# Alibi attention and feed-forward on one core: q and k of the last nine blocks turned by transposing DMA

## The chip, the core and the metric

The kernel runs on one core of one Trainium2 chip. The core has five engines with instruction queues of their own: TensorE (PE in the profile; its weight loads are shown as PEld), VectorE (DVE), ScalarE (ACT), GpSimd (POOL) and SyncE (SP). SP does no arithmetic here; it issues DMAs and runs its queue strictly in order, as every engine does. POOL issues the loads that change the type from fp32 to fp16 on the way, and computes two tiny operations a block. Sixteen DMA engines move the data for all queues.

The metric is the time of one execution on the device, in microseconds (us). The kernel before took 323.11 us, the median of three runs (322.46 to 323.45).

## The reference

For 8 batches, 8 heads, 576 positions and a head width of 64 the reference computes sliding-window attention with linear position biases, joins the heads to rows of 512, and puts each row through a normalisation and a two-layer network with a residual:

```python
scores = scale * np.matmul(q, k.transpose(0, 1, 3, 2))
bias = slopes[:, None, None] * (-np.abs(rel).astype(np.float32))[None, :, :]
mask = (rel >= 0) & (rel < window)               # window = 128
scores = np.where(mask, scores + bias[None], -1000000000.0)
attn = softmax(scores)                           # over the keys
x = matmul(attn, v) -> (batch, 576, 512)
xn = (x - mean) / np.sqrt(var + 1e-06) * g_ln
out = x + np.maximum(xn @ w_ch1, 0.0) @ w_ch2    # 512 -> 2048 -> 512
```

## The kernel before

**Blocks.** Two batches form a pair, p = 0 to 3. A pair has nine blocks of 128 rows: blocks 0 to 7 are positions 0 to 511, alternately of the one and the other batch, and block 8 (T) holds the last 64 positions of both. In the order of work the 36 blocks are numbered n = 9p + blk. The last nine, n = 27 to 35, are those of pair 3.

**Attention of a block.** POOL loads raw q and k of two blocks at a time (load_qk, L207 to L218) and v of one (load_v, L220). A partition of the raw tile takes two neighbouring positions, so that a piece read is 512 bytes. For the scores q and k must lie with the head's 64 elements on the partitions. That is what `turn(p, i)` does (L283): TensorE transposes 64 by 64 pieces into PSUM (L277; 64 of them for two blocks, 32 for a T block), here into the two banks that otherwise take the scores (ps_sc), and DVE and ACT each copy one bank's q (L296) and k (L297) to SBUF. k is put back in natural order by the copy's stride. q stays in another order, even positions first; the masks (L52 to L54) and the output (L868 to L873: two DMAs a block, one for even and one for odd rows) are made to fit it. `attend` (L367) then multiplies k by q (L393), ACT takes the exponential of the whole bank (L401), and DVE multiplies by the decay and the mask (L412). A block needs two such calls (one for blocks 0 and 1 of a pair). `seen` (L353) leaves out the queries that a key half cannot see, from block n = 8 on: half of the products have 64 columns then, and before it all have 128. `values` (L428) multiplies by v (L445) and divides by the sum on DVE (L453, L454).

**Normalisation.** From n = 8 on, DVE takes the moments (L542, L543), POOL makes the reciprocal root from them (L497, L500), DVE makes the centred rows xc (L484, `normal`), and a transposing DMA on SP (L492) writes them to xT, the operand of the first layer.

**The network.** Blocks are taken in groups: six of two blocks and then six of four (GROUPS, L26), g = 0 to 11. Group 8 holds n = 20 to 23. `mlp1` (L668) is the first layer: 16 units of four products L677, each drained by ACT (L693). `mlp2` is the second layer of the groups of two; `fast_mlp2` (L747) is that of the groups of four, which works with seven products of half-size matrices (L776) in 14 units of eight products, sums of which DVE builds (L745) and adds (L794).

**What sets the order.** PE, ACT and DVE run in the order in which the program is written. The attention of later blocks is cut into steps and woven into the network: `weave_at` names the unit of the network after which the next step is put (L911 to L915 for groups 6 to 11). Four steps belong to a block n: the turn of a later block pair (n + 3, L642), values of n and scores of n + 2, masks and moments, and `normal`. In groups 6 to 11 the first layer takes steps after units 0, 2, 5, 7, 8, 10, 13, 15 and the second after units 1, 3, 6, 7, 7, 9, 12, 13; the turns stand at 5 and 13 and at 6 and 12. SP and POOL are not written out: a planner orders their queues by when it expects an instruction's inputs. The first layer of a group needs xT of all its blocks: the fourth block's `normal` is put after unit 3 of the second layer before.

**Buffers.** Raw q and k have four tiles each (raw_pool), turned q and k three (turned_pool): a new tile waits until the last user of the old one is through.

Of the kernel before, what the change touches and what calls it, by code (L numbers as in the profile page):

```python
# [10 lines left out]
FP16 = mybir.dt.float16  # L11
# [6 lines left out]
P = 128  # L18
# [7 lines left out]
GROUPS = [2] * 6 + [4] * 6  # L26
FAST = 6

NV = 10
AHEAD = 6  # L30

FIRST_GROUPS, FIRST = 2, 4
# [6 lines left out]
def distances():  # L39

    key = np.arange(P)[:, None]
    query = np.arange(P)[None, :]

    def far(rel, ok=True):
        return np.where(ok & (rel >= 0) & (rel < WINDOW), rel, FAR)

    ends = [far(P + query - HALF * b - key, query // HALF == b) for b in range(2)]  # L50
    tail = far(query - key, query // HALF == key // HALF)
    evens_first = np.r_[0:P:2, 1:P:2]  # L52
    both = [far(P + query - key), far(query - key)]
    cols = [m[:, evens_first] for m in both] + [*ends, tail]  # L54
    return np.concatenate(cols, axis=1).astype(np.float16)


# [1 line left out]
def kernel(  # L59
# [22 lines left out]
        return ctx.enter_context(tc.tile_pool(name=name, bufs=bufs, **kw))  # L82

    consts = pool("consts", 1)
    raw_pool = pool("raw", 4)
    turned_pool = pool("turned", 3)
    probs_pool = pool("probs", 4)
    own_pool = pool("own", 2)
    x_pool = pool("x", 7)
# [34 lines left out]

    g_sb = consts.tile([P, NKB], FP32)
    nc.sync.dma_start(out=g_sb, in_=moe_g_ln.rearrange("(kb p) -> p kb", p=P))
    g_line = consts.tile([1, DM], FP32)
    nc.sync.dma_start(out=g_line, in_=moe_g_ln.rearrange("(o d) -> o d", o=1))
    g_row = consts.tile([P, DM], FP32)
# [9 lines left out]
    QF, QD = NFB // 2, DM // 2  # L139
    hsum = [consts.tile([P, QF, 2 * P], FP16, name=f"hs{i}", tag=f"hs{i}") for i in range(2)]  # L140
    spare = [w1[:, i, :].rearrange("p (f d) -> p f d", d=QD) for i in range(4)]
    hsum.append(spare[3])
    vext = [
# [60 lines left out]

    raw = {}

    def load_qk(src, tag, p, i):  # L207

        n = min(P, S - i * P)
        t = raw_pool.tile([P, H, 2, D], FP16, tag=tag, name=tag)  # L210
        raw[tag, p, i] = t
        for b in range(2):
            nc.gpsimd.dma_start(  # L213
                out=t[b * n // 2 : (b + 1) * n // 2],
                in_=src[2 * p + b, :, i * P : i * P + n, :].rearrange(
                    "h (c r) d -> c h r d", r=2
                ),
            )  # L218
# [64 lines left out]
    def turn(p, i, in_sc=False, copies=(nc.vector.tensor_copy, nc.scalar.copy)):  # L283

        ps = [bank(b if in_sc else None) for b in range(2)]
        k = keys_tile("k", p, i)  # L290
        if i < 4:
            q = queries(p, i)
            transposed("q", p, i, [t[:, 0] for t in ps])
            transposed("k", p, i, [t[:, 1] for t in ps])
            for b, copy in enumerate(copies):
                copy(out=q[:, b], in_=ps[b][:, 0])  # L296
                copy(out=k[:, b].rearrange("p h (c r) -> p r h c", r=2), in_=ps[b][:, 1])  # L297
        else:
            q = keys_tile("q", p, i)
            for tag, t, dst, copy in zip("qk", ps, (q, k), copies):  # L300
                transposed(tag, p, i, [t[:, 0]])
                copy(out=dst[:, 0].rearrange("p h (c r) -> p r h c", r=2), in_=t[:, 0])

    def bank(sc=None):
        if sc is None:
            return ps_mm.tile([P, 2, 2, HP, HALF], FP16, tag="mm", name="ps_tr")
        return ps_sc[sc][:, 0].bitcast(FP16).rearrange(
            "p (t r h c) -> p t r h c", t=2, r=2, h=HP
        )

    def queries(p, i):
        t = turned_pool.tile([P, 2, 2, HP, HALF], FP16, tag="q", name="q")
        turned["q", p, i] = t.rearrange("p b r h c -> p b h r c")
        return t

    def keys_tile(tag, p, i):
        t = turned_pool.tile([P, 2, HP, P], FP16, tag=tag, name=tag)
# [2 lines left out]

    def turn_first():

        q, k = queries(0, 0), keys_tile("k", 0, 0)
        ps = [bank(b)[:, 0] for b in range(2)]
        transposed("q", 0, 0, ps)
        for b in range(2):
            nc.vector.tensor_copy(out=q[:, b], in_=ps[b])
# [18 lines left out]
        return t  # L346

    weights_of, unmasked, scored = {}, {}, []

    def in_halves(t):  # L350
        return t if len(t.shape) == 3 else t.rearrange("p (r c) -> p r c", r=2)

    def seen(p, blk, o, t):  # L353


        both, every = slice(0, 2), slice(0, HALF)
        first, second = slice(0, HALF // 2), slice(HALF // 2, HALF)
        if p == 0 and blk < SEEN:
            return [(0, both, every), (1, both, every)]
        if blk == T:  # L360
            batches = [slice(0, 1), slice(1, 2)]
            return [(c, batches[c if o == T else t], every) for c in range(2)]
        if o == blk:
            return [(0, both, every), (1, both, second)]
        return [(1, both, every), (0, both, first)]

    def attend(p, blk, keys, mask, tag, hps):  # L367

        heads = slice(2 * hps[0], 2 * hps[-1] + 2)
# [9 lines left out]
        scored.append((p, blk))  # L383
        ps = banks.rearrange("p j (n t q) -> p j n t q", n=len(hps), t=nk)
        qt, b = turned["q", p, blk // 2], blk % 2
        for n, hp in enumerate(hps):
            for t, o in enumerate(keys):
                kt = turned["k", p, o // 2][:, o % 2]
                for c, r, queries in seen(p, blk, o, t):
                    cols = slice(c * HALF, (c + 1) * HALF)  # L390
                    for j in range(2):
                        rows = slice(j * HALF, (j + 1) * HALF)
                        nc.tensor.matmul(  # L393
                            in_halves(ps[cols, j, n, t, :])[:, r, queries],
                            kt[rows, hp, cols],
                            in_halves(qt[rows, b, hp])[:, r, queries],
                            start=True,
                            stop=True,
                        )
        dst = pr[:, heads].rearrange("p h t q -> p h (t q)")  # L400
# [239 lines left out]
    for n in range(8, count):  # L640
        first_half, second_half = values_steps(n)
        steps.append(  # L642
            turn_step(n + 3, True) if n + 3 < count and order[n + 3][1] % 2 == 0 else []
        )
        step = first_half + second_half[:1]
        if n + 1 < count and order[n + 1][1] == T:
            step += [(scores_tail, order[n][0])]
        if n + 2 < count:
            step += scores_step(n + 2)
        steps.append(step)  # L650
        steps.append(
            [m for t in (n + 1, n + 2) if t < count for m in masks_of(t)] + [(stats, n)]
        )
        steps.append([(normal, n)])
# [207 lines left out]
    def store(p, blk, o, cols=slice(0, DM), queues=(nc.sync,)):  # L862
        queues = cycle(queues)
        for b, t0, w, p0 in spans(p, blk):
            dst, src = out[b, t0 : t0 + w, cols], o[p0 : p0 + w, cols]
            if blk == T:
                next(queues).dma_start(out=dst, in_=src)
            else:  # L868
                dst = dst.rearrange("(c r) d -> r c d", r=2)
                for r in range(2):  # L870
                    next(queues).dma_start(
                        out=dst[r], in_=src[r * HALF : (r + 1) * HALF]
                    )  # L873

    def weave_at(units, *places, also=()):
        for u, _ in enumerate(units):
# [16 lines left out]
    with tc.manual_schedule(engines={engine.PE}):  # L893
        with tc.manual_schedule(engines={engine.Activation, engine.DVE}):
# [16 lines left out]
            for g in range(6, len(GROUPS)):  # L911
                weave_at(
                    mlp1(g), 0, 2, 5, 7, 8, 10, 13, 15, also=(1, 4) if g == 6 else ()
                )
                weave_at(fast_mlp2(g), 1, 3, 6, 7, 7, 9, 12, 13)  # L915
    assert done == len(steps)


# [28 lines left out]
```

## Time and profile before

| | |
|---|---|
| median of three runs | 323.11 us (322.46 to 323.45) |
| the profiled execution's own time | 322.94 us |
| its span | 321.1 us |
| granted TensorE clock | 1.00 throughout |
| PE busy | 307.5 us, 96% of the span |
| DVE busy | 233.4 us, 73% |
| ACT busy | 184.6 us, 57% |
| POOL busy | 114.9 us, 36% |
| DMA packets of the loads on POOL's queue | 79,872, 18.36 MB |
| DMA packets of SP's queue | 21,810, 13.05 MB |

The span is the profiled stretch from the first to the last instruction; 1.8 us of the execution's own time lie outside it. Busy is the time in which an engine had at least one instruction running. "Releaser" names what ended an engine's idle time. A time stamp such as 183.78 is us from the span's start. The chain of waits is the profile's list of the work that ended last, followed back from the end, in order of time. For a DMA the profile shows the time that its engine spent on issuing it and the time from the start of the issue to landing, when the data are there and the semaphore is raised.

### The profile page before, as it was taken

The numbers are of one execution on the slowest core, as the hardware profiler recorded it, in microseconds if no ns is written. First come the engines' busy times: TensorE is split into PE (matmuls) and PEld (weight loads), VectorE is DVE, ScalarE is ACT, GpSimd is POOL, SyncE is SP. The second block draws the span as 40 slices with busy tenths as digits, with TensorE's granted clock in tenths as the row PEclk, the third lists the DMA queues.
The fourth block names the chain that finished last, engine by engine and source line by source line (L and its number), as shares of the span: only waits on it lengthen the run. The fifth ranks groups of instructions, "written<-read, shape, count | busy, mean of one in ns | idle before, by whom it ended". The sixth has DMA issues, their size and how long they took to land.

```text
span 321.1 us, 10472 instructions
## 1 busy us (share of the span) xinstructions
PE 307.5 (96%) x4478; PEld 207.3 (65%) x4478; DVE 233.4 (73%) x556; ACT 184.6 (57%) x320; POOL 114.9 (36%) x188
## 2 busy tenths in 40 slices
PE   8889999999899999999999999999999999999993
PEld 2478655758558576545875587558755874685582
DVE  2788878786687788758994899579958984761462
ACT  6588756666558466478248824873488247405600
POOL 8833657769145264534252534220000001000000
PEclk9999999999999999999999999999999999999999
DMA  9999999999999899895389769660340134015005
GB/s 113 169 206 196 190 142 189 186 115 184 59 118 120 78 143 92 89 160 55 45 108 160 68 68 115 117 51 18 84 85 18 18 68 98 18 32 117 0 2 131
DMA packets 102048, 32.34 MB, mean 101 GB/s; under 512 B 92913, under 2 KB 97649, under 8 KB 102002
## 3 DMA queue, kind: packets, MB, share of 16 engines
q0 software_dynamic: 79872, 18.36, 66.7%
q1 hardware_dynamic: 21810, 13.05, 19.5%
q8 instruction: 35, 0.57, 0.8%
q10 hardware_dynamic: 320, 0.26, 0.4%
q14 instruction: 11, 0.09, 0.1%
HBM read 36.90 MB, written 9.44 MB: 144 GB/s over the span
## 4 chain that ended last, share of the span: by engine, by line
PE 76%; DVE 10%; ACT 5%; POOL 3%; DMA 2%; issue 2%; POOLq 0%; ACTq 0%
PE ps_r L677 24%; PE ps_r L776 21%; PE ps_m L710 10%; PE ps_m L677 9%; PE ps_sc L393 4%; ACT probs L401 3%; PE ps_sc L277 2%; PE ps_r L445 2%; DVE probs L412 2%; DMA k<-in_k_dram 2%; PE ps_pv L445 2%; DVE st L542 1%; POOL rstd L500 1%; POOL q L213 1%; DVE o L852 1%
## 5 line engine op out<-in xcount | busy, mean ns | idle before, releaser
L677 PEld LDWEIGHTS <-w1g 128*128 128x128 f16 x640 | 60.0, 98 | 48.9 <-issue 1.8
L677 PE MATMUL ps_r<-xT,w1g 128*128 128x512 f16 x384 | 85.5, 379 | 0.0
L401 ACT ACTIVATE probs<-ps_sc 128x1024 f16<-128x1024 f32 x56 | 54.3, 1027 | 35.5 <-PE ps_sc L393 35.5
L693 ACT ACTIVATE ht<-ps_r 128x512 f16<-128x512 f32 x96 | 56.2, 600 | 30.6 <-PE ps_r L677 30.4
L497 POOL TENSOR_TENSOR rstd<-moments,powers 128x1 f32<-128x1 f32 x28 | 5.4, 193 | 118.5 <-DVE moments L543 118.4
L710 PE MATMUL ps_m<-w,ht 128*128 128x512 f16 x192 | 46.0, 380 | 0.0
L776 PE MATMUL ps_r<-w,ht 128*128 128x256 f16 x384 | 44.1, 273 | 0.0
L223 POOL DMA_DIRECT2D vx<-in_v_dram x40 | 34.6, 879 | 22.4 <-PE ps_r L445 9.7
L412 DVE TENSOR_TENSOR probs<-probs,m 128x1024 f16<-128x1024 f16 x56 | 37.3, 688 | 6.5 <-ACT probs L401 6.3
L776 PEld LDWEIGHTS <-ht 128*128 128x128 f16 x384 | 37.1, 98 | 4.7
L693 ACT ACTIVATE ht<-ps_m 128x256 f16<-128x256 f32 x91 | 33.1, 388 | 8.6 <-PE ps_m L677 6.0
L213 POOL DMA_DIRECT2D q<-in_q_dram x40 | 27.4, 692 | 14.4 <-PE ps_sc L277 6.6
L677 PE MATMUL ps_m<-xT,w1g 128*128 128x256 f16 x256 | 31.4, 273 | 1.1 <-ACT ht L693 0.8
L213 POOL DMA_DIRECT2D k<-in_k_dram x40 | 26.8, 684 | 6.7 <-DMA w<-in_moe_w_ch_dram 3.1
L710 PEld LDWEIGHTS <-ht 128*128 128x128 f16 x192 | 17.1, 98 | 17.4
L484 DVE TENSOR_SCALAR xc<-x,moments,rstd 128x512 f16<-128x512 f16 x28 | 11.5, 412 | 20.0 <-POOL rstd L500 19.0
L542 DVE BATCH_NORM_STATS2 st<-x 128x6 f32<-128x512 f16 x36 | 24.6, 684 | 0.0
L393 PE MATMUL ps_sc<-q,k 64*64 64x128 f16 (+1 forms) x1088 | 20.2, 208 | 3.9 <-DVE k L297 1.3
L296 ACT COPY q<-ps_sc 128x512 f16<-128x512 f16 x15 | 8.8, 586 | 25.1 <-PE ps_sc L277 24.9
L776 PE MATMUL ps_r<-w,hs 128*128 128x256 f16 x192 | 22.5, 273 | 0.0
L445 PEld LDWEIGHTS <-probs 128*128 128x128 f16 x448 | 18.7, 97 | 4.7 <-DVE probs L412 0.3
L393 PEld LDWEIGHTS <-k 64*64 64x64 f16 x1088 | 15.2, 107 | 8.9 <-issue 6.5
(85 smaller groups left out, 390.7 us busy)
## 6 DMA issues: line engine op xcount, KB each, us to landing
out_dram<-o SPq DMA_DIRECT2D x68, 128.0 KB, 2.5
q<-in_q_dram POOLq DMA_DIRECT2D x32, 128.0 KB, 4.5
k<-in_k_dram POOLq DMA_DIRECT2D x32, 128.0 KB, 5.8
vx<-in_v_dram POOLq DMA_DIRECT2D x32, 128.0 KB, 7.6
w<-in_moe_w_ch_dram POOLq DMA_DIRECT2D x8, 512.0 KB, 12.2
q<-in_q_dram POOLq DMA_DIRECT2D x8, 64.0 KB, 4.8
k<-in_k_dram POOLq DMA_DIRECT2D x8, 64.0 KB, 4.3
vx<-in_v_dram POOLq DMA_DIRECT2D x8, 64.0 KB, 6.0
```

What stands on the lines that cost most here:

```text
L213: nc.gpsimd.dma_start(out=t[b * n // 2 : (b + 1) * n // 2], in_=src[2 * p + b, :, i * P : i * P + n, :].rearrange("h (c r) d -> c h r d", ...
L223: nc.gpsimd.dma_start(out=vx[p0 : p0 + n, :, 0:D], in_=v[b, :, t0 : t0 + n, :].rearrange("h p d -> p h d"),)
L393: nc.tensor.matmul(in_halves(ps[cols, j, n, t, :])[:, r, queries], kt[rows, hp, cols], in_halves(qt[rows, b, hp])[:, r, queries], start=Tr ...
L401: nc.scalar.activation(out=dst.rearrange("p (n j) q -> p j n q", j=2), in_=ps.rearrange("p j n t q -> p j n (t q)"), func=AF.Exp, scale=in ...
L412: nc.vector.tensor_tensor(out=dst, in0=dst, in1=mask, op=ALU.mult)
L445: nc.tensor.matmul(ps[:, i, :], pr[:, h, t, :], vext[(p * NSLOT + o) % NV][:, h, :], start=(n == 0), stop=(n == len(terms) - 1),)
L484: nc.vector.tensor_scalar(out=xc, in0=xs[order[n]], scalar1=moments[:, n, 0:1], scalar2=rstd[:, n : n + 1], op0=ALU.subtract, op1=ALU.mult,)
L542: nc.vector.bn_stats(out=st, in_=xs[order[n]])
L677: nc.tensor.matmul(ps[:, 0:cols], w[:, kb, fb * P : (fb + 1) * P], xT[:, kb, 0:cols], start=(kb == 0), stop=(kb == NKB - 1),)
L693: nc.scalar.activation(out=ht[:, fb, 0:cols], in_=ps[:, 0:cols], func=AF.Relu)
L710: nc.tensor.matmul(sums[at], ht[:, fb, at * P : (at + 1) * P], w2[:, fb, :], start=(fb == 0), stop=(fb == NFB - 1),)
L776: nc.tensor.matmul(banks[name][pair][:, pair, :], lhs[:, fb, pair * P : (pair + 1) * P], rhs[:, fb, :], start=(first and fb == 0 and (pair ...
```

## The change

1. **The turn of pair 3.** For p >= 3 (`by_dma`) `load_qk` puts natural rows into the raw tile: a piece read is 64 numbers, as for v. `turn` issues transposing DMAs on SP instead of products on PE and copies on DVE and ACT: for two blocks two DMAs for q and two for k, each 128 by 512, for T one each, 18 in all. The turn is written one block sooner, at n + 4.
2. **Natural order of queries everywhere.** The masks lose their even-first order. The copies of q in the turns that stay on PE use the stride that only k's had. `seen` names one contiguous half of 64 queries instead of 32 of the even and 32 of the odd. A block's output is one DMA of 128 rows; a store's round of queues starts at SP, so that such a block has its whole store on SP, in the last group too, where the two halves had gone to SP and ACT.
3. **`junk`.** After a turn in the score banks, the next call of `attend` in that bank computes all 128 queries of each key half; `seen` applies again from the call after.
4. **Places.** In the second layers of groups 6 to 11 steps move from unit 6 to 5 and from 12 to 11: these are the turns.
5. **Buffers.** turned_pool has four tiles; g_line and g_row share memory with the sums of the second layer.

```diff
+BY_DMA_TURN = 3
...
-    evens_first = np.r_[0:P:2, 1:P:2]
     both = [far(P + query - key), far(query - key)]
-    cols = [m[:, evens_first] for m in both] + [*ends, tail]
+    cols = [*both, *ends, tail]
...
-    turned_pool = pool("turned", 3)
+    turned_pool = pool("turned", 4)
...
+            if by_dma(p):
+                nc.gpsimd.dma_start(
+                    out=t[:, b] if i < 4 else t[b * n : (b + 1) * n, 0],
+                    in_=src[2 * p + b, :, i * P : i * P + n, :].rearrange(
+                        "h p d -> p h d"
+                    ),
+                )
+                continue
...
+        q, k = (keys_tile(tag, p, i) for tag in "qk")
+        if by_dma(p):
+            for tag, dst in (("q", q), ("k", k)):
+                src = raw.pop((tag, p, i))
+                for b in range(2 if i < 4 else 1):
+                    nc.sync.dma_start_transpose(
+                        out=dst[:, b], in_=src[:, b].rearrange("p h d -> p (h d)")
+                    )
+            return
...
             for b, copy in enumerate(copies):
-                copy(out=q[:, b], in_=ps[b][:, 0])
-                copy(out=k[:, b].rearrange("p h (c r) -> p r h c", r=2), in_=ps[b][:, 1])
+                for t, dst in enumerate((q, k)):
+                    copy(
+                        out=dst[:, b].rearrange("p h (c r) -> p r h c", r=2),
+                        in_=ps[b][:, t],
+                    )
...
-        if p == 0 and blk < SEEN:
+        if junk[len(scored) % 2] or p == 0 and blk < SEEN:
             return [(0, both, every), (1, both, every)]
...
         if o == blk:
-            return [(0, both, every), (1, both, second)]
-        return [(1, both, every), (0, both, first)]
+            return [(0, both, every), (1, slice(1, 2), every)]
+        return [(1, both, every), (0, slice(0, 1), every)]
...
-            turn_step(n + 3, True) if n + 3 < count and order[n + 3][1] % 2 == 0 else []
+            [
+                f
+                for m in (n + 3, n + 4)
+                if m < count and order[m][1] % 2 == 0 and by_dma(order[m][0]) == (m == n + 4)
+                for f in turn_step(m, True)
+            ]
...
-            if blk == T:
-                next(queues).dma_start(out=dst, in_=src)
-            else:
-                dst = dst.rearrange("(c r) d -> r c d", r=2)
-                for r in range(2):
-                    next(queues).dma_start(
-                        out=dst[r], in_=src[r * HALF : (r + 1) * HALF]
-                    )
+            next(queues).dma_start(out=dst, in_=src)
...
-                weave_at(fast_mlp2(g), 1, 3, 6, 7, 7, 9, 12, 13)
+                weave_at(fast_mlp2(g), 1, 3, 5, 7, 7, 9, 11, 13)
```

More of the change, by code (lines that the diff above doesn't have):

```diff
@@ L27 @@
 FAST = 6
-NV = 10
+NV, RAW = 10, 4
+BY_DMA_TURN = 3
 AHEAD = 6
@@ L84 @@
     consts = pool("consts", 1)
-    raw_pool = pool("raw", 4)
-    turned_pool = pool("turned", 3)
+    raw_pool = pool("raw", RAW)
+    turned_pool = pool("turned", 4)
     probs_pool = pool("probs", 4)
@@ L126 @@
     nc.sync.dma_start(out=g_sb, in_=moe_g_ln.rearrange("(kb p) -> p kb", p=P))
-    g_line = consts.tile([1, DM], FP32)
+    QF, QD = NFB // 2, DM // 2
+    hsum = [consts.tile([P, QF, 2 * P], FP16, name=f"hs{i}", tag=f"hs{i}") for i in range(2)]
+    g_line, g_row = (
+        t.rearrange("p f d -> p (f d)")[:, 0 : 2 * DM].bitcast(FP32) for t in hsum
+    )
+    g_line = g_line[0:1]
     nc.sync.dma_start(out=g_line, in_=moe_g_ln.rearrange("(o d) -> o d", o=1))
-    g_row = consts.tile([P, DM], FP32)
     one_line = consts.tile([1, P], FP32)
@@ L138 @@
     w2 = consts.tile([P, NFB, DM], FP16)
-    QF, QD = NFB // 2, DM // 2
-    hsum = [consts.tile([P, QF, 2 * P], FP16, name=f"hs{i}", tag=f"hs{i}") for i in range(2)]
     spare = [w1[:, i, :].rearrange("p (f d) -> p f d", d=QD) for i in range(4)]
@@ L205, with by_dma @@
     raw = {}
+    def by_dma(p):
+        return p >= BY_DMA_TURN
     def load_qk(src, tag, p, i):
@@ L211, in load_qk @@
         raw[tag, p, i] = t
+        if by_dma(p):
+            t = raw[tag, p, i] = t.rearrange("p h r d -> p (h r d)").rearrange(
+                "p (b h d) -> p b h d", b=2, h=H
+            )
         for b in range(2):
+            if by_dma(p):
[6 more added lines that the diff above has]
+                continue
             nc.gpsimd.dma_start(
@@ L283, in turn @@
     def turn(p, i, in_sc=False, copies=(nc.vector.tensor_copy, nc.scalar.copy)):
+        q, k = (keys_tile(tag, p, i) for tag in "qk")
+        if by_dma(p):
+            for tag, dst in (("q", q), ("k", k)):
[3 more added lines that the diff above has]
+                        out=dst[:, b], in_=src[:, b].rearrange("p h d -> p (h d)")
+                    )
+            return
         ps = [bank(b if in_sc else None) for b in range(2)]
-        k = keys_tile("k", p, i)
         if i < 4:
-            q = queries(p, i)
             transposed("q", p, i, [t[:, 0] for t in ps])
@@ L295, in turn @@
             for b, copy in enumerate(copies):
-                copy(out=q[:, b], in_=ps[b][:, 0])
-                copy(out=k[:, b].rearrange("p h (c r) -> p r h c", r=2), in_=ps[b][:, 1])
+                for t, dst in enumerate((q, k)):
+                    copy(
+                        out=dst[:, b].rearrange("p h (c r) -> p r h c", r=2),
+                        in_=ps[b][:, t],
+                    )
         else:
-            q = keys_tile("q", p, i)
             for tag, t, dst, copy in zip("qk", ps, (q, k), copies):
@@ L306, in bank @@
             return ps_mm.tile([P, 2, 2, HP, HALF], FP16, tag="mm", name="ps_tr")
+        junk[sc] = True
         return ps_sc[sc][:, 0].bitcast(FP16).rearrange(
@@ L309, in bank @@
         )
[L311 to L314, printed above, removed]
     def keys_tile(tag, p, i):
@@ L321, in turn_first @@
     def turn_first():
-        q, k = queries(0, 0), keys_tile("k", 0, 0)
+        q, k = (keys_tile(tag, 0, 0) for tag in "qk")
         ps = [bank(b)[:, 0] for b in range(2)]
@@ L326, in turn_first @@
         for b in range(2):
-            nc.vector.tensor_copy(out=q[:, b], in_=ps[b])
+            nc.vector.tensor_copy(
+                out=q[:, b].rearrange("p h (c r) -> p r h c", r=2), in_=ps[b]
+            )
         ps_row = spread_g()
@@ L348 @@
     weights_of, unmasked, scored = {}, {}, []
+    junk = [False, False]
     def in_halves(t):
@@ L356, in seen @@
         both, every = slice(0, 2), slice(0, HALF)
-        first, second = slice(0, HALF // 2), slice(HALF // 2, HALF)
-        if p == 0 and blk < SEEN:
+        if junk[len(scored) % 2] or p == 0 and blk < SEEN:
             return [(0, both, every), (1, both, every)]
@@ L382, in attend @@
         banks = ps_sc[len(scored) % 2]
-        scored.append((p, blk))
         ps = banks.rearrange("p j (n t q) -> p j n t q", n=len(hps), t=nk)
@@ L399, in attend @@
                         )
+        junk[len(scored) % 2] = False
+        scored.append((p, blk))
         dst = pr[:, heads].rearrange("p h t q -> p h (t q)")
```

## The prediction, made before the changed kernel ran

> **What bounds the kernel now.** I read the busy shares first, then the chain of waits, then PE's instructions in order of time, and last the queues of SP and POOL around the place that decides.
>
> ```profile
> PE 307.5 (96%) x4478; PEld 207.3 (65%) x4478; DVE 233.4 (73%) x556; ACT 184.6 (57%) x320; POOL 114.9 (36%) x188
> ```
>
> PE has work running in 307.5 of 321.1 us; what shortens its queue shortens the kernel, and what makes it wait lengthens it. The chain of waits, where the turns of pair 3 stand (start, us, what):
>
> ```profile
> 183.84 6.23 PE ps_r L776 x56
> 190.06 0.64 PE ps_sc L277 x64
> 190.71 0.98 PE ps_r L776 x8
> ...
> 222.50 0.02 issue
> 222.52 0.58 ACT q L296
> 223.11 0.65 ACT k L297
> 223.75 0.04 issue
> 223.79 0.54 PE ps_sc L393 x18
> ```
>
> A turn stands on PE's own chain. PE in order of time gives a turn's full price: 32 products of the first layer with a turn among them, and 32 without.
>
> ```profile
> 198.86 5.35 PE L677 MATMUL ps_r<-xT,w1g 128*128 128x512 f16 x24
> 204.14 0.45 PE L277 MATMUL ps_sc<-iden,q 64*64 64x64 f16 x32
> 204.42 0.51 PE L277 MATMUL ps_sc<-iden,k 64*64 64x64 f16 x32
> 204.86 1.90 PE L677 MATMUL ps_r<-xT,w1g 128*128 128x512 f16 x8
> 206.59 0.23 PE L445 MATMUL ps_r<-vx,probs 128*128 128x65 f16 x2
> ...
> 207.76 7.08 PE L677 MATMUL ps_r<-xT,w1g 128*128 128x512 f16 x32
> 214.68 0.42 PE L445 MATMUL ps_r<-vx,own 128*128 128x65 f16 x8
> ```
>
> From the first product to the values it is 206.59 - 198.86 = 7.73 us with the turn and 214.68 - 207.76 = 6.92 without: 0.81 us. A transposing DMA that has the queues to itself (issued at 179.97) and one beside loads (199.20), issue and landing:
>
> ```profile
> L492 SPq DMA_TRANSPOSE xT<-xc x1: 1202/1202/1202, 180.0 to 180.0; - x1
> DMA to landing us min/median/max: 2.4/2.4/2.4
> ```
> ```profile
> L492 SPq DMA_TRANSPOSE xT<-xc x1: 1220/1220/1220, 199.2 to 199.2; - x1
> DMA to landing us min/median/max: 4.3/4.3/4.3
> ```
>
> SP pays 1.2 us to issue either. The spread comes after it: the trace's packet records give 0.79 us from first to last packet for the first (512 packets, no load packets in between) and 1.77 us for the second (910 load packets in between); 2.4 is 1.20 + 0.79 and 0.4 to the semaphore.
>
> **The change part by part.** The sum is made against the profiled execution's own 322.94 us (span 321.1 and 1.8 around it); the median of the runs shown, 323.11, is 0.17 above it, well within their spread.
>
> *Five turns leave PE.* By the same subtraction they cost 0.75 (at 190.0; 64 products of the second layer without a turn take 284.62 - 277.63 = 6.99), 0.81, 0.76, 0.74 and 0.74 us: **-3.8**. The wait at 223.79 behind ACT's copies goes too: from values to scores 0.54 us there, 0.35 at 214.68: **-0.2**. The copies on DVE (0.42 + 0.72 us a turn) and ACT (0.59 + 0.75) vanish beside PE's work and count nothing.
>
> *`junk`.* Two attend calls after each of the nine turns of pairs 1 and 2 compute everything. The chain shows a block's scores at 0.57 us before n = 8, where all is computed (41.53), and at 0.47 after (230.17): 0.10 a turn, and 0.1 more for one T block, whose scores take 0.38: **+1.0** (bounds 0.8 and 1.1).
>
> *q copies with a stride.* DVE needs 722 ns with the stride (L297) and 421 without (L296), ACT 745 and 586: +0.30 and +0.16 us a copy in every turn left. It costs where PE waits for the copies: at 16.60 (two on ACT, 0.32), 37.71, 89.30, 121.57, 151.09 and 166.63 (DVE, 0.30 each): **+1.8** (bounds 0, if the next wait shrinks by as much, and 2.0 with the one at 101.43). The earlier place of the turn before 166.63 wins nothing: DVE is busy with L794 until it starts those copies. Turns in other second layers than that one belong to pair 3 or stand before group 6.
>
> *Stores.* A block's two issues (0.55 to 0.6 us each) become one: SP is freed of some 17 us and given 18 x 1.2 = 21.6 us. In the last group SP has four issues at the end before and after: 0 (bounds -0.6 and +0.6, an issue). Buffers and shared memory: 0; the user of g_row is long through. `seen` names as many columns as before, 64 in one piece for twice 32: 0.
>
> *Loads of pair 3.* With 64-number pieces a load has the form of v's: 879 instead of 692 ns on POOL, 1024 instead of 512 packets, 16 full and 4 small loads. POOL idles most of this stretch; packets matter below.
>
> *Eighteen transposes on SP.* That is where it is decided. I read the order in which the changed kernel's instructions stand on SP, as built:
>
> ```
> xT n=20, two stores, two stores, xT n=21, xT n=22,
> q x2, k x2 (blocks 27, 28); q x2, k x2 (29, 30); q x2 (31, 32),
> xT n=23, k x2 (31, 32), three stores, xT n=24 ...
> ```
>
> xT of n = 23, the last that group 8's first layer needs, stands behind ten new transposes, and these behind xT of n = 22. Before, it was issued at 190.58 us (SP idle ahead of it) and its reader came at 198.86. Now:
> - xT of n = 22 is issued at 179.97; the new ones follow from 181.17, the first packets at 182.36. Their inputs are there: raw data loaded long before, old readers through by 183.8.
> - The reader comes at 198.86 - 0.75 (no turn at 190) = 198.1.
> - With r us a transpose, xT of n = 23 lands at 182.36 + 10 r + 0.79 + 0.42 (itself taken as undisturbed). At SP's pace, r = 1.2, that is 195.6: no wait. At r = 1.77 it is **201.3: PE waits 3.2 us**. At r = 2.34 it is 207.0: 8.9 us.
>
> Which r? In the same microseconds POOL loads the raw tile of blocks 33 and 34, since a turn on PE has just freed it:
>
> ```profile
> 181.11 1.42 POOL L213 DMA_DIRECT2D q<-in_q_dram  x2 [1.62 <-PE ps_sc L277]
> 182.51 1.38 POOL L213 DMA_DIRECT2D k<-in_k_dram  x2
> 183.85 0.92 POOL L223 DMA_DIRECT2D vx<-in_v_dram  x1
> 189.14 0.19 POOL L497 TENSOR_TENSOR rstd<-moments,powers 128x1 f32<-128x1 f32 x1 [4.36 <-DVE moments L543]
> ```
>
> In the changed kernel these are 4 x 1024 + 1024 packets, and 2048 more for T behind them. Seven transposes of the trace met 500 or more load packets: 1.75, 1.77, 1.77, 2.34, 2.63, 3.05 and 3.07 us, with some 700 load packets in each; 7168 packets cover ten such transposes. I take 1.77, the row 20 us from the place and with packets of the new loads' size; ends are 1.2 and 2.34 (the mean and median of the seven).
>
> A rule stands against these rows: the Trainium skill (Advanced Engine Details and Errata, X-Bar Transpose) says that transpose DMAs "are as fast as regular DMAs", and its page DMA: Bandwidth & Descriptors (Rules for kernel authors) that a transpose next to ordinary DMAs "needs nothing". By it r stays 1.2 and the sum is that of the second case below. The trace agrees for a transpose alone (0.79 us), not beside loads.
>
> *POOL behind SP.* T's loads now reuse the raw tiles of blocks 27 and 28, so they wait for four of the new transposes, and on POOL the reciprocal root of n = 23 (189.14 before) is queued behind them. At r = 1.77 the fourth lands at 182.36 + 4 x 1.77 + 0.42 = 189.9, two k loads of some 0.7 us follow, and L500: DVE's xc at about 192.5 instead of 190.14. DVE then holds back L794, but within the 3.2 us that PE waits anyway.
>
> Sum: 322.94 - 3.8 - 0.2 + 1.0 + 1.8 + 3.2 = **324.9 us**.
>
> **The rivals.**
> 1. *No wait (the other side).* The engines alternate fairly between the queues and ten transposes run at SP's pace. For it: SP's issue is 1.2 us even beside loads, and 0.79 us of transfer leaves room. Against: no transpose met 500 load packets and took less than 1.75 us. It decides at r = 1.45, where the landing meets the reader: 322.94 - 1.2 = **321.7**, ends 319.9 (no copy on PE's path) and 321.9.
> 2. *Only POOL's detour.* Transposes take about 1.5 us, and what PE loses is DVE held by the late root. DVE's slack there is some 2 us (L794 at 192.01, needed by a product at 194.3); a root 2.5 to 3.5 us late costs about 1.3: **323.0**.
> 3. *Sharing as at the worst.* r = 3.05 as at 168.66 us, beside this very kind of load batch: landing at 214.1, a wait of 16 us: **337.7**. Against: its packets ran in a stretch with stores too. The Trainium skill (VectorE: DVE Perf Modes, The three transpose paths) gives 1309 ns for a 128x128 by DMA against 390 on TensorE and advises TensorE where PSUM will do; by that a 128x512 is estimated at 5.2 us and the wait at over 40. The 0.79 us of the trace speak against that figure, not against its direction.
>
> **How the numbers follow.** My forecast, a wait of 2.4 us or more, gets 0.50; no wait 0.33; the detour 0.14; the worst 0.03. About 0.3%, 1 us, can be told from no change here: faster means below 322.1, slower above 324.1. No wait gives faster 0.28 and same 0.05; the detour faster 0.04, same 0.08, slower 0.02; the forecast same 0.01 and slower 0.49; the worst slower 0.03. Together 0.32, 0.14, 0.54. The forecast's own range is 324.1 to 330.6 (r = 2.34). The whole reaches from 320.5, just under the case without a wait, to 329.5.
>
> **What the changed profile would show.** PE's first-layer products of group 8, at about 198 us, wait for a DMA into xT by some 3 us; that transpose lands 12 us or more after its xc is written. Ten transposes stand on SP from about 181 us, 1.2 us apart, each landing 4 us or more after its issue. No L277 after 181 us; PE loses 0.75 us at each of five places. Scores after a turn take 0.57 us; waits of scores for DVE's copies grow by 0.3. POOL's root of n = 23 comes two us later. I am wrong if PE meets no wait near 198, or if the first layers of groups 9 to 11 wait too, whose xT stand behind fewer new transposes and have 6 us and more to spare.

## The result and the profile after

The changed kernel takes 328.0 us (median of six runs, 327.1 to 330.0) against 323.2 of the kernel before on the same chip: 1.016 times, 95% interval 1.0128 to 1.0193. It is 4.8 us slower; the forecast, 324.9, was 1.8 above the median of the kernel before. The profiled execution of the changed kernel took 327.94 us (span 326.1), that of the kernel before 322.94 (span 321.1): the two traces differ by the same 5 us and can be compared piece by piece.

The busy shares of the changed kernel:

```profile
PE 305.8 (94%) x4190; PEld 206.3 (63%) x4190; DVE 231.5 (71%) x547; ACT 180.9 (55%) x311; POOL 118.5 (36%) x188
```

PE has 288 instructions and 1.7 us of work fewer, and the span is longer: what was lost is idle time. PE's list of waits has a new head (us in all, times, longest):

```profile
PE ps_r L806 <- DVE o L824: 5.0, 1, 5.0
```

One single wait of 5 us. PE in order of time shows its place (L806 here is L776 before, L707 is L677):

```profile
194.24 0.45 PE L416 MATMUL ps_sc<-q,k 64*64 64x64 f16 x32
199.71 3.56 PE L806 MATMUL ps_r<-w,w 128*128 128x256 f16 x16 [5.02 <-DVE o L824]
203.08 3.68 PE L806 MATMUL ps_r<-w,ht 128*128 128x256 f16 x32
206.59 0.65 PE L470 MATMUL ps_r<-vx,probs 128*128 128x65 f16 x16
207.17 0.54 PE L416 MATMUL ps_sc<-q,k 64*64 64x64 f16 x32
207.64 7.08 PE L707 MATMUL ps_r<-xT,w1g 128*128 128x512 f16 x32
```

PE stands still in the second layer of group 7, ahead of a product whose bank DVE has not emptied, and not at the first layer of group 8 (207.64, no wait). The 16 products behind the wait take 3.56 us; 16 such products take 1.92 in the runs below where no wait precedes them. The chain of waits, in excerpts, says who was late:

```profile
183.90 4.99 DMA q<-in_q_dram
188.89 6.94 DMA k<-k
...
196.39 1.36 POOL k L223 x2
197.75 0.22 POOL rstd L522
...
198.05 0.57 POOL rstd L525
...
198.65 0.06 DVE xc L509
...
198.97 0.69 DVE o L824
```

Read from the end: DVE adds (L824) only after it has written xc, which waits for the root on POOL (L525), which stands behind two loads of k (L223), which wait for a turning DMA of k that landed at 195.8. POOL's own order of time has both waits in brackets, 4.46 and 2.20 us:

```profile
192.81 1.38 POOL L223 DMA_DIRECT2D q<-in_q_dram  x2 [4.46 <-DMA q<-q]
196.39 1.36 POOL L223 DMA_DIRECT2D k<-in_k_dram  x2 [2.20 <-DMA k<-k]
197.75 0.22 POOL L522 TENSOR_TENSOR rstd<-moments,powers 128x1 f32<-128x1 f32 x1
```

And SP's, with the ten turning DMAs ahead of xT of n = 23, and that xT's time to landing:

```profile
182.76 1.19 SPq L517 DMA_TRANSPOSE xT<-xc  x1
184.12 3.32 SPq L311 DMA_TRANSPOSE q<-q  x2
187.60 2.56 SPq L311 DMA_TRANSPOSE k<-k  x2
190.36 2.50 SPq L311 DMA_TRANSPOSE q<-q  x2
193.45 2.74 SPq L311 DMA_TRANSPOSE k<-k  x2
196.37 2.50 SPq L311 DMA_TRANSPOSE q<-q  x2
199.09 1.19 SPq L517 DMA_TRANSPOSE xT<-xc  x1
```
```profile
L517 SPq DMA_TRANSPOSE xT<-xc x1: 1189/1189/1189, 199.1 to 199.1; - x1
...
DMA to landing us min/median/max: 4.8/4.8/4.8
```

xT lands at 203.9, with its reader at 207.64: the wait behind POOL's root had put the reader off by more than xT was late.

The last view is busy time by windows; its third number from the end, under PEclk, is the clock that PE was granted:

```profile
core 0: us, PE busy (x) PEld busy (x) DVE busy (x) ACT busy (x) POOL busy (x), PEclk, DMA share, GB/s
...
194.70:199.70 5.00, 0.00 (x0) 0.01 (x1) 1.05 (x3) 1.92 (x2) 3.08 (x5) 1.00 1.65 184
199.70:203.00 3.30, 3.29 (x16) 2.30 (x16) 3.23 (x8) 0.00 (x0) 0.00 (x0) 0.50 1.34 146
```

After the 5 us of idleness the clock is 0.50 for 3.4 us by the trace's clock records (199.70 to 203.11). That is why 16 products took 3.56 us: 1.64 more than at full clock.

Where the 5.0 us of span come from can be followed product by product, since the two kernels have the same products in the same order once those of the turns are left out. PE is 2.89 us late when group 7's second layer begins (186.67 against 183.78). The first turn left out brings that down to 2.16. Behind the wait and the slow products it is 8.76 (203.08 against 194.32): 5.0 for the wait and 1.6 for the clock. The four other turns, with a wait that went with one of them, bring it down to 5.55, the lateness of DVE's last three additions (320.51 against 314.96). The span ends only 5.0 later, so 0.55 come back at the end. In sum 2.89 + 6.60 - 3.94 - 0.55 = 5.00.

### The profile page after: what moved, and what is told of

The parts are those of the page before. It is cut to its first block, busy times and chain, and to the rows that moved or that the text cites. A ratio compares the mean times of both kernels' runs of the same rounds, so it can differ in the third digit from the quotient of the medians.

```text
span 326.1 us, 9870 instructions
## 1 busy us (share of the span) xinstructions
PE 305.8 (94%) x4190; PEld 206.3 (63%) x4190; DVE 231.5 (71%) x547; ACT 180.9 (55%) x311; POOL 118.5 (36%) x188
## 4 chain that ended last, share of the span: by engine, by line
PE 69%; DVE 9%; DMA 8%; POOL 5%; ACT 5%; issue 2%; POOLq 0%; ACTq 0%
PE ps_r L707 23%; PE ps_r L806 19%; PE ps_m L740 10%; PE ps_m L707 8%; DMA w<-in_moe_w_ch_dram 4%; PE ps_sc L416 4%; ACT probs L426 3%; DMA k<-k 2%; PE ps_r L470 2%; DVE probs L437 2%; DMA q<-in_q_dram 2%; PE ps_pv L470 1%; PE ps_sc L294 1%; DVE st L567 1%; POOL vx L240 1%
## 5 line engine op out<-in xcount | busy, mean ns | idle before, releaser
L707 PEld LDWEIGHTS <-w1g 128*128 128x128 f16 x640 | 60.3, 98 | 49.0 <-issue 1.7
L707 PE MATMUL ps_r<-xT,w1g 128*128 128x512 f16 x384 | 85.1, 380 | 0.0
L806 PE MATMUL ps_r<-w,ht 128*128 128x256 f16 x384 | 44.1, 273 | 0.0
L806 PEld LDWEIGHTS <-ht 128*128 128x128 f16 x384 | 37.2, 98 | 4.9
L707 PE MATMUL ps_m<-xT,w1g 128*128 128x256 f16 x256 | 31.3, 273 | 1.0 <-ACT ht L723 0.7
L416 PE MATMUL ps_sc<-q,k 64*64 64x128 f16 (+1 forms) x1088 | 21.2, 211 | 5.3 <-DVE k L321 1.9
L230 POOL DMA_DIRECT2D q<-in_q_dram x30 | 20.5, 691 | 12.0 <-PE ps_sc L294 3.1
L416 PEld LDWEIGHTS <-k 64*64 64x64 f16 x1088 | 15.8, 107 | 10.5 <-issue 8.2
L230 POOL DMA_DIRECT2D k<-in_k_dram x30 | 20.1, 685 | 5.2 <-DMA w<-in_moe_w_ch_dram 4.3
L806 PE MATMUL ps_r<-w,hs 128*128 128x256 f16 x192 | 21.9, 273 | 0.0
L426 ACT ACTIVATE own<-ps_sc 128x1024 f16<-128x1024 f32 x12 | 11.9, 1029 | 15.5 <-PE ps_sc L416 14.3
```

The lines of the kernel that those rows point to most:

```text
L230: nc.gpsimd.dma_start(out=t[b * n // 2 : (b + 1) * n // 2], in_=src[2 * p + b, :, i * P : i * P + n, :].rearrange("h (c r) d -> c h r d", ...
L416: nc.tensor.matmul(in_halves(ps[cols, j, n, t, :])[:, r, queries], kt[rows, hp, cols], in_halves(qt[rows, b, hp])[:, r, queries], start=Tr ...
L426: nc.scalar.activation(out=dst.rearrange("p (n j) q -> p j n q", j=2), in_=ps.rearrange("p j n t q -> p j n (t q)"), func=AF.Exp, scale=in ...
L707: nc.tensor.matmul(ps[:, 0:cols], w[:, kb, fb * P : (fb + 1) * P], xT[:, kb, 0:cols], start=(kb == 0), stop=(kb == NKB - 1),)
L806: nc.tensor.matmul(banks[name][pair][:, pair, :], lhs[:, fb, pair * P : (pair + 1) * P], rhs[:, fb, :], start=(first and fb == 0 and (pair ...
```

## The experiments

Two theories. **P**: what is late is the root on POOL, which stands behind loads that wait for turning DMAs; SP's queue is only a part of it. **S**: what is late is xT on SP behind ten turning DMAs, as the forecast had it. Medians are compared with the kernel before on the same chip (323.2 to 323.4 us). PE's waits for the first loads, at 12 to 15 us, take up to 2.2 us in the traces (0.8 in the kernel before). So the traces are also compared without the start: from the first product of PE's turn at about 36 us to the end of the span. That comparison rests on one trace of each kernel.

| kernel | median us | ratio to before (95%) | from the turn to the end, us | against before |
|---|---|---|---|---|
| before | 323.2 | | 321.1 - 35.81 = 285.29 | |
| changed | 328.0 | 1.0160 (1.0128 to 1.0193) | 326.1 - 36.65 = 289.45 | +4.16 |
| own_raw | 323.99 | 1.0016 (0.9988 to 1.0044) | 322.1 - 35.49 = 286.61 | +1.32 |
| sp_manual | 328.91 | 1.0163 (1.0131 to 1.0196) | 327.7 - 35.52 = 292.18 | +6.89 |
| own_sp | 320.84 | 0.9920 (0.9892 to 0.9948) | 319.1 - 36.35 = 282.75 | -2.54 |
| own_warm | 322.88 | 0.9984 (0.9965 to 1.0003) | 321.8 - 35.74 = 286.06 | +0.77 |
| pe_turn | 325.64 | 1.0066 (1.0045 to 1.0087) | 323.5 - 35.69 = 287.81 | +2.52 |
| pe_nojunk | 325.94 | 1.0055 (1.0030 to 1.0081) | 325.0 - 38.02 = 286.98 | +1.69 |
| pe_contig | 322.19 | 0.9959 (0.9937 to 0.9980) | 320.7 - 35.88 = 284.82 | -0.47 |
| mix | 321.50 | 0.9957 (0.9926 to 0.9988) | 320.4 - 37.06 = 283.34 | -1.95 |
| mix_sp | 319.52 | 0.9887 (0.9840 to 0.9933) | 316.9 - 35.49 = 281.41 | -3.88 |

**own_raw: the loads no longer wait for turning DMAs.** The last block T of pair 3 gets raw tiles of its own, so its loads need no tile that a turning DMA must free; the planner then also puts them much earlier on POOL, at 56 to 59 us.

```diff
-        t = raw_pool.tile([P, H, 2, D], FP16, tag=tag, name=tag)
-        raw[tag, p, i] = t
-        if by_dma(p):
+        if by_dma(p) and i == 4:
+            t = raw[tag, p, i] = consts.tile([P, 1, H, D], FP16, name="rt" + tag, tag="rt" + tag)
+        else:
+            t = raw_pool.tile([P, H, 2, D], FP16, tag=tag, name=tag)
+            raw[tag, p, i] = t
+        if by_dma(p) and i < 4:
```

> The changed kernel, but raw q and k of pair 3's T block have tiles of their own, so their loads on POOL no longer wait for four transposes, and the reciprocal root of n = 23 no longer stands behind them; the ten transposes ahead of xT of n = 23 on SP stay. Theory P (the 5.0 us wait of PE at 194.7 and the half clock after it come through POOL: load behind transpose, root behind load, DVE behind root, PE behind DVE): the root of n = 23 comes within 1 us of its moments, the wait behind L824 is gone, and 6.7 us come back: 321.3 us if nothing takes its place. Theory S (SP's queue, the first of the prediction): with the root on time, xT of n = 23 lands at about 203.2 us of the changed kernel's clock against a reader at 201.0, so a wait of about 2.3 us for that DMA appears at the first layer of group 8: 323.6 us, or 325 if the clock halves after it. Theory C (the stall is contention on the DMA engines and any queue order has it): a wait of 4 us or more remains near the same place, 326 to 328 us.

Measured: 323.99 us, 4 less than the changed kernel. The wait behind L824 (here L827) is gone and another, of 2.14 us, has come forward at the first layer of group 8:

```profile
193.48 1.92 PE L809 MATMUL ps_r<-w,w 128*128 128x256 f16 x16
...
199.31 0.54 PE L419 MATMUL ps_sc<-q,k 64*64 64x64 f16 x32
201.99 8.75 PE L710 MATMUL ps_r<-xT,w1g 128*128 128x512 f16 x32 [2.14 <-DVE own L440]
```

The engine named in brackets need not be what ended it. xT of n = 23 was issued at 197.97 and took 3.8 us to land, 201.8:

```profile
197.97 1.22 SPq L520 DMA_TRANSPOSE xT<-xc  x1
...
DMA to landing us min/median/max: 3.8/3.8/3.8
```

Two of the runs below bear this out: with xT earlier the wait is gone (own_sp), and products that use the same bank but not xT start without a wait (own_warm). So P holds for the 5 us and theory C does not, and S's wait lay beneath it, at the place that the forecast named and with two thirds of its 3.2 us. The first layer behind it takes 8.75 us instead of 7.08, again at half clock (0.50 from 202.4 to 205.8).

The edit also takes the packets of T's loads out of this stretch. That is not what helped: the four turning DMAs at the head of the queue need as long as in the changed kernel, 9.8 us from first to last packet against 9.7.

**sp_manual: a short queue on SP, the loads as in the change.** SP's instructions stand in program order; four turning DMAs instead of ten are ahead of xT of n = 23, and T's loads still wait for those four.

```diff
-    with tc.manual_schedule(engines={engine.PE}):
+    with tc.manual_schedule(engines={engine.PE, engine.SP}):
```

> The changed kernel with SyncE's instructions in program order: four turning DMAs (blocks 27 and 28) stand ahead of xT of position 23 on SyncE instead of ten; GpSimd's two pairs of loads still stand ahead of the root of the norm of 23 and still wait for those four. Theory P (what delays the first layer of group 8 is the root on GpSimd, behind loads that wait for the turning DMAs): the wait of 5.0 us behind L824 stays within 1 us of that, the products behind it run at half clock again (about 1.6 us lost), and the time is 326.5 to 328.5 us. Theory S (what delays it is the length of SyncE's queue ahead of xT): the wait and the half clock go, 328.0 - 5.0 - 1.6 = 321.4 us.

Measured: 328.91 us, no better than the changed kernel. POOL's loads still wait for a turning DMA, and PE's wait is there with nearly the same length:

```profile
196.82 1.36 POOL L223 DMA_DIRECT2D k<-in_k_dram  x2 [2.97 <-DMA k<-k]
...
200.15 3.57 PE L806 MATMUL ps_r<-w,w 128*128 128x256 f16 x16 [5.55 <-DVE o L824]
203.52 4.83 PE L806 MATMUL ps_r<-w,ht 128*128 128x256 f16 x32
```

The half clock lasts two stretches here (the 32 products behind take 4.83 instead of 3.66 us). Against the kernel before it stands where the changed kernel does (1.0163 and 1.0160), and it is 0.4 us over the range that P gave. Without the start its trace is 2.73 us longer: 0.53 in the wait, 1.16 at half clock, and 1.05 lost before 183.7 us, whose cause stays open. SP's queue alone does not cause the 5 us.

**own_sp: both queues cleared.** The edits of the two experiments together.

> The kernel with tiles of their own for T's rows, and SyncE in program order as well: neither the root nor xT has a long queue ahead of it. The trace of the run with tiles of their own kept a wait of 2.14 us ahead of the first layer of group 8 and lost 1.67 us to half clock behind it. Theory P and S together (two queues, one behind the other): no wait over 0.5 us between 190 and 205 us, a clock of 1.00 there, and 323.99 - 2.14 - 1.67 = 320.2 us. If that remaining wait has nothing to do with SyncE's order (the landing of xT among other traffic, say), it stays and the time is 323.5 to 324.5 us.

Measured: 320.84 us, 2.5 us faster than the kernel before. xT is issued at 193.19, and PE runs through the place without a wait and at a clock of 1.00:

```profile
193.19 1.20 SPq L520 DMA_TRANSPOSE xT<-xc  x1
...
194.34 1.92 PE L809 MATMUL ps_r<-w,w 128*128 128x256 f16 x16
...
200.18 0.54 PE L419 MATMUL ps_sc<-q,k 64*64 64x64 f16 x32
200.65 7.08 PE L710 MATMUL ps_r<-xT,w1g 128*128 128x512 f16 x32
```

From own_raw to own_sp the trace without the start loses 3.86 us; the wait of 2.14 and the clock's 1.67 are 3.81. By the medians SP's order alone (sp_manual) brought nothing, the tiles alone (own_raw) 4.0 us, and SP's order another 3.2 once the tiles were there. The two waits lie one behind the other.

**own_warm: is it the idle time that halves the clock?** Eight products on a constant tile fill the wait of own_raw.

```diff
             ps = psum("ps_m1")
+            if g == 8 and u == 0:
+                for _ in range(8):
+                    nc.tensor.matmul(ps, ones[:, 0:P], ones, start=True, stop=True)
             for kb in range(NKB):
```

> The kernel with tiles of their own for T's rows, and ahead of the first product of group 8's first layer eight products of 512 columns on a constant tile, into the bank that this first product overwrites: they change no result and fill some 1.7 us of the 2.14 us in which TensorE waited there. Theory W (the idle time of 2.14 us makes the clock fall to half, and that costs the 1.67 us behind it): the clock stays at 1.00 between 199 and 208 us, the 32 products take 7.1 instead of 8.75 us, and the time is 323.99 - 1.67 = 322.3 us. Rival (the clock falls for another reason, or the products are slow from traffic): 0.5 again in the windows there, and 323.5 to 324.5 us.

Measured: 322.88 us, 1.1 less than own_raw, and between the two expectations. This run was on another chip, and the intervals of the two ratios overlap, so the times alone do not decide. The trace is plainer:

```profile
199.98 1.90 PE L711 MATMUL ps_r<-ones 128*128 128x512 f16 x8
203.37 7.07 PE L713 MATMUL ps_r<-xT,w1g 128*128 128x512 f16 x32 [1.49 <-issue]
```

xT was late by a little more here (SP issued it at 199.17 instead of 197.97, so that filling and remaining wait are 3.39 us together), but the clock stayed at 1.00 and the 32 products took 7.07 us. Without the start the trace is 0.55 shorter, about the 1.67 less at half clock and the 1.25 more of waiting. The granted clock of the other runs points the same way. A slow stretch of 3.4 us costs half of that, 1.7 of 322 us, so that the mean clock of a run falls to 0.995 or less. Eight of the ten runs of own_raw stand there, and three of the twelve of own_warm, though only in the traced ones is it known where the stretch lay; the two of own_raw that kept 0.998 and more are its fastest, 322.59 and 322.65 us.

So keeping PE at work helps, but the length of one wait does not alone decide. The clock halved behind waits of 5.55, 5.02, 2.14 and, in pe_nojunk at 14.79 us, 2.21 us, and not behind 1.70 (mix at 201.23 us) and 1.49. Yet in mix it also halved at 14.84 us, behind two waits of 0.36 and 1.21 us with two small products between them; the last three numbers of these lines are clock, DMA share and GB/s:

```profile
12.00:16.00 4.00, 2.43 (x67) 1.27 (x53) 3.47 (x16) 1.57 (x4) 3.47 (x5) 0.85 1.66 170
16.00:20.00 4.00, 3.21 (x59) 2.00 (x58) 1.66 (x4) 3.14 (x6) 1.45 (x3) 0.72 1.25 209
```

**pe_turn, pe_nojunk, pe_contig: the parts that are not the DMA.** In pe_turn no pair is turned by DMA; everything else of the change stays. pe_nojunk also drops the line that makes the attend after a turn compute everything. pe_contig copies q without the stride again, so its queries stand evens first where the masks and the output take them in natural order: it computes wrong rows, and only its time is read.

```diff
-BY_DMA_TURN = 3
+BY_DMA_TURN = 4
...
-        junk[sc] = True
...
-                for t, dst in enumerate((q, k)):
-                    copy(
-                        out=dst[:, b].rearrange("p h (c r) -> p r h c", r=2),
-                        in_=ps[b][:, t],
-                    )
+                flat = q[:, b].rearrange("p h q -> p (h q)")
+                copy(
+                    out=flat.rearrange("p (r h c) -> p r h c", r=2, h=HP),
+                    in_=ps[b][:, 0],
+                )
+                copy(
+                    out=k[:, b].rearrange("p h (c r) -> p r h c", r=2), in_=ps[b][:, 1]
+                )
```

> The changed kernel with every turn on PE (the limit for turning by DMA is set past the last pair); natural order, one store a block, the earlier places and junk stay. Theory E (junk and the strided copies cost what the prediction's rows say, 0.1 us a turn and 0.3 us where PE waits for a copy): fourteen turns, 2.8 us for pairs 0 to 2 as the time stamps at 167 to 170 us show, 0.6 of junk and 0.3 of copies more in pair 3, and 0.5 us less at the end of the kernel: 326.4 us, no wait behind L824, clock 1.00. Rival N (the 2.8 us by which the changed kernel is late at 170 us is mostly the start of that one run, where loads landed later): 324.9 us or less.

> As pe_turn, but the calls after a turn skip the unseen queries as all others do. Theory E: fourteen turns x 0.10 us and 0.1 more for each of two T blocks less than pe_turn: 1.6 us less, 324.8 us; scores after a turn take 0.47 us on PE. Rival: the extra columns hide beside other work: no difference.

> As pe_nojunk, but the copies of q write in the order in which the transposes leave them, even positions first, as in the kernel before. The masks and the stores stay in natural order, so the attention is that of the wrong queries; the amount of work is the same. Theory E: 0.3 us back at each of six or seven places where PE waits for these copies: 2.0 us less than pe_nojunk, 322.8 us, which is the kernel before and 0.4 us less at its end; the waits of PE for DVE's copies are those of the kernel before. Rival: DVE and ACT have the time, and the place of the copies does not matter: 324.8 us.

Measured: 325.64, 325.94 and 322.19 us: 0.8 under, 1.1 over and 0.6 under what was expected. By the medians `junk` costs nothing that can be told (the intervals of the first two overlap widely, and the expected gain did not show), and the stride 3.75 us. The traces say where that is too simple: the profiled run of pe_nojunk waits 2.21 us for the first k and then runs its warm-up at half clock, so that it reaches the turn at 38.02 instead of 35.7 us. Without the start `junk` is worth 0.83 us, over fourteen turns, and the stride 2.16. The granted clocks show that other runs stumbled in the same way: six of the ten of pe_nojunk have 0.993 or less, while eight of ten of pe_turn and of pe_contig keep 0.996 or more. Among the runs with 0.996 or more the medians are 325.55, 324.69 and 322.16 us, which makes `junk` 0.9 and the stride 2.5. So much of what the stride seems to cost by the medians is a chance of the start. The stride itself is plain in the groups of copies (line, tile, count, then busy us and mean ns of one), DVE and then ACT, in pe_nojunk:

```profile
L321 DVE COPY q<-ps_sc 128x512 f16<-128x512 f16 x13 | 9.5, 728 | 5.2 <-PE ps_sc L294 5.2
...
L321 ACT COPY q<-ps_sc 128x512 f16<-128x512 f16 x15 | 11.0, 734 | 23.7 <-PE ps_sc L294 23.4
```

and in pe_contig:

```profile
L321 DVE COPY q<-ps_sc 128x512 f16<-128x512 f16 x13 | 5.5, 420 | 5.8 <-PE ps_sc L294 5.8
...
L321 ACT COPY q<-ps_sc 128x512 f16<-128x512 f16 x15 | 8.8, 587 | 22.9 <-PE ps_sc L294 22.5
```

PE's waits for DVE's copy at the scores are 2.6 us in pe_nojunk and 1.3 in pe_contig. So 2.4 of the changed kernel's 4.8 us are lost by pe_turn already, with every turn on PE, and turning pair 3 by DMA as the change does it loses the rest.

**mix and mix_sp: only the part that pays.** The kernel before, with evens-first queries, its two stores, its cheap copies and no `junk`; pair 3 alone is turned by DMA, with its q loaded evens first by two DMAs of 64 partitions, T in tiles of its own, and the change's four turned tiles and shared memory. mix leaves SP to the planner, mix_sp puts SP in program order.

```diff
+                if tag == "q" and i < 4:
+                    rows = rows.rearrange("h (c r) d -> r c h d", r=2)
+                    for r in range(2):
+                        nc.gpsimd.dma_start(
+                            out=t[r * HALF : (r + 1) * HALF, b], in_=rows[r]
+                        )
...
-    with tc.manual_schedule(engines={engine.PE}):
+    with tc.manual_schedule(engines={engine.PE, engine.SP}):
```

> The kernel before (queries evens first, two stores a block, the cheap copies of its q, its places for the turns in second layers), with pair 3 alone turned by DMA: its q is loaded evens first by two DMAs, T's rows have tiles of their own, and SyncE's order is the planner's. If the sum of parts holds: the kernel before 323.2, less 4.0 for the five turns taken off TensorE, plus the wait of 2.1 and the half clock of 1.7 that the run with tiles of their own still had: 323.0 us. If turning by DMA itself costs TensorE more than the turns that it saves (loads that come late, transfers that slow one another), the time is over 324 us.

> The same mixed kernel with SyncE in program order, so that four turning DMAs instead of ten stand ahead of xT of position 23. If the sum of parts holds, wait and half clock are gone as well: 323.2 - 4.0 = 319.2 us, faster than the kernel before. If the transfers themselves, and not their order, delay xT: 322 to 323.5 us.

Measured: 321.50 and 319.52 us. mix waits 1.70 us for xT, and the clock holds:

```profile
201.23 7.07 PE L719 MATMUL ps_r<-xT,w1g 128*128 128x512 f16 x32 [1.70 <-DMA xT<-xc]
```

Without the half clock's 1.7 us its expected 323.0 is 321.3, close to what was measured; four of its ten runs, the traced one among them, have a clock of 0.994 or less all the same (in the traced one from the half clock at 14.84 us), and the six others have a median of 321.0. mix_sp has no wait there, and is faster than both kernels, by 1.1% (0.7 to 1.6, from four runs) than the kernel before. Without the start its trace gains 3.88 us, against the 4.0 that five turns were to save: with nothing else in the way, turning by DMA is worth the whole of what it takes from PE.

## Why the prediction was right or wrong

The direction and the range were right; the size was not, and of the two mechanisms beside each other the wrong one was given the price. By the prediction's own sign, a wait of group 8's first layer for xT, its mechanism was wrong: that layer did not wait. That 328.0 lies within 324.1 to 330.6 is in part luck, since the range was made of lengths of that wait.

- *Five turns leave PE, -4.0*: right, and in its parts. Product by product the five turns take 0.73 to 0.78 us each off PE, 3.7 together, and the wait for ACT's copies another 0.21; mix_sp gains 3.88.
- *`junk` +1.0 and the stride +1.8*: 2.9 us at the beginning of group 7's second layer look like a hit on 2.8, but 0.84 of them are there at 36.65 us already: 0.07 at the first k, 0.2 at the strided copies, and some 0.5 in the first layer at 24 to 27 us, where PE waits for ACT and for a load of w. Behind that it is 2.05 us. The jumps at the copies' places sum to 1.6 (0.22 at 16.6 us, 1.38 behind it), so the stride was about right. Some 0.6 remain for `junk`, which was sized too large: 0.83 for fourteen turns is 0.06 a turn, not 0.10.
- *Stores 0, bounds -0.6 and +0.6*: -0.55 at the end of the span, just within the bounds.
- *Eighteen transposes on SP, 3.2 us at r = 1.77*: the mechanism was there, masked. From the first packet of the ten to the landing of xT behind them it is 18.5 us, 1.68 for each of the eleven. own_raw uncovered a wait of 2.14 us at the place named.
- *POOL behind SP*: **this step failed.** It let the fourth turning DMA land at 189.9 and xc be written at 192.5, and hid what was left "within the 3.2 us that PE waits anyway". Two things were wrong in it. First, it used one pace for all ten, and took the spread of a transpose's packets for the whole time until the next one. From the first packet (185.35) to the fourth landing (195.83) it was 10.5 us, where the prediction has 4 x 1.77 + 0.42 = 7.5; the other six and xT needed 8.0, 1.15 each. The spread was sized well: taken 512 at a time in order of time, the packets of the four spread over 2.6, 1.4, 1.3 and 2.0 us, 1.8 in the mean. What the prediction left out are the gaps between one and the next, 1.6, 0.5 and 0.4 us. The first four ran beside the loads of blocks 33 and 34 (POOL issued them from 183.9 to 188.4); that these made the gaps is likely, but no run takes the loads away. So the fourth landed at 195.8 instead of 189.9: 3.0 us are the later beginning of the row (185.35 against 182.36), and 3.0 are this slower pace. Second, the wait that comes first on PE takes the cover from nothing: the product held by L824 comes 6.3 us of work ahead of the reader of xT (own_sp: 194.34 to 200.65), so a late root is paid before xT's lateness counts, and swallows that lateness, not the reverse. POOL's root came at 197.75 instead of 189.14 + 2.9 = 192.04, 5.7 us late, and PE paid 5.02 of that.
- *Not in the sum at all*: 1.64 us at half clock behind the wait. own_warm showed that this loss goes when PE is kept at work.
- The second rival (only the detour) had the right place and a quarter of the price (1.3 us). It presumed a root 2.5 to 3.5 us late, and a slack on DVE of some 2 us, read at the second addition behind xc (192.01). The first one ended at 191.15 and freed the bank for the product at 192.56, which comes 0.75 us sooner without the turn. That leaves 0.7 us, and 0.7 of the 5.7 us were not paid. The time of the first rival, no wait, is near that of own_sp, where both queues are cleared: 320.84, against 321.7.
- The third rival's estimate of a wait of over 40 us is 38 by the prediction's own formula; the longest time from issue to landing in the row was 8.0 us.

In one line: 322.94 + 2.9 + 5.0 + 1.6 - 3.9 - 0.55 = 328.0, where the forecast had 322.94 + 2.8 + 3.2 - 4.0.

## What to carry to other kernels

When a change puts transfers ahead of something on a queue, follow every other queue that waits for those transfers too, and price the wait that comes first in the order of the engine that bounds, since it swallows the later one. Price a stretch of transfers by the time from one to the next, gaps and landing included, and not by the packets of one. And check a sum of small parts one by one: here the part that was the point of the change was worth all of its 4 us, and a layout that came with it and the reuse of one buffer gave more than that away.

## What the runs showed of the hardware that was not expected

- PE's clock halves after a short idleness. The slow stretches in the traces last 3.41 us, and twice that in sp_manual (6.83), where the first began 1 us before PE went on. 1.64 us were lost behind 5.02 us of waiting and 1.67 behind 2.14; after 1.70 and 1.49 us nothing was lost. A wait of a little over 2 us thus cost nearly twice its length. In mix the clock halved at 14.84 us behind no wait longer than 1.21, so the traces give no limit for a single wait. The Trainium skill (TensorE: Matmul & The Clock Gate, Part 1) puts the fall to half at one idle window or more, of about 3.4 us, and says that the windows run freely. The slow stretches here agree with that length; that 2.14 us of idleness were enough does not agree with a whole idle window.
- A transposing DMA of 128x512 spreads its packets over 0.79 us alone, over 1.3 to 2.6 for the first four of the row beside the loads and 0.6 to 1.6 for the next six, and lands 3.6 to 8.0 us after its issue (median 5.7 for the first eleven turning DMAs). SP spent 1.19 to 2.01 us on issuing one of these, not always the prediction's 1.2. The Trainium skill's sentence that transpose DMAs "are as fast as regular DMAs" (Advanced Engine Details and Errata, X-Bar Transpose) was taken as a rule for r beside loads; no run here sets a regular DMA of this size beside such loads, so whether the sentence holds there is not shown. The words "needs nothing", which the prediction quotes from the Trainium skill (DMA: Bandwidth & Descriptors, Rules for kernel authors), stand there in a row on which transfers must be serialized so that they do not corrupt each other, and say nothing of speed.
